# An S5 state-space mixer gated by an MLP: time steps on partitions replaced by states on partitions, a scan along time, and table GELU

## The chip, the cores and the metric

The kernel runs on one core of one Trainium2 chip. The metric is the device time of one execution in microseconds (us). The span of a profile is a little shorter than the time of the same execution (206.1 against 207.9 us in the changed kernel). TensorE does the matmuls (816 in the changed kernel's trace), VectorE, ScalarE and GpSimd the elementwise work (306, 163 and 142 instructions), SyncE issues most transfers (67 of the 77 listed there). In profile lines they are PE (with PEld for weight loads), DVE, ACT, POOL and SP. The program gives each engine its own queue of instructions in a fixed order, and an instruction that waits there holds up what stands behind it: in run 1 VectorE waited 8.2 us for a transpose that stood behind waiting matmuls in TensorE's queue. Every run is marked fast or slow. The slow ones are kept out of all ratios: one execution of run 5 (granted clock 0.73 instead of about 0.91), one of run 8 (210.74 us), and two of the kernel before (253.97 and 255.09 us). They are left out of the times quoted here, too.

## The reference

The input is 2048 tokens of 448 features. Both branches read the normalized token; the result is `x + s * silu(MLP)`.

```python
xn = layernorm(x)
# A: a diagonal complex recurrence over time, 448 states
Lam_bar = exp(dt * Lam)
Bu = xn @ (((Lam_bar - 1) / Lam)[:, None] * Bmat).T   # per token
h[t] = Lam_bar * h[t-1] + Bu[t]                     # 2048 steps
s = 2 * real(h @ Cmat.T) + xn * Dskip
# B: LayerNorm again, then 448 -> 1792 -> 448
m = gelu_tanh(layernorm(xn) @ w1 + b1) @ w2 + b2
out = x + s * silu(m)
```

## The kernel before

Both kernels work through groups of 512 tokens (four tiles of 128), and both fix the order of every engine's queue when they are built, from a list schedule with estimated durations. These parts matter.

```python
# recurrence inside 128 tokens: decay by tables, then a triangular matmul as prefix sum
def CS(t, ri):                       # x32 (16 tiles, real and imaginary)
    for pti in range(4):
        matmul(bk[:, pti*128:(pti+1)*128], Bs_sb[:, bb, ri, pti*128:...], Ub)   # 128x128
def CHAIN(t):                        # carry from tile to tile: four small GpSimd operations
    ...
def SE(t, ri):                       # eviction of each state block, carry added: 128 ScalarE operations
    for pt in range(4):
        act(S_sb[..., pt, ...], bk[:, pt*128:...], Identity, bias=vst[:, t, ri, pt:pt+1])

# GELU of each 128x512 block: ScalarE, then VectorE x3, ScalarE, VectorE
a  = act(bank, Identity, bias=b1)            # GA
u  = dve(a * a); q = dve(u * K + 1); w = dve(q * a)      # GU, GQ, GW
sg = act(w, Sigmoid, scale=2C)               # GS
gT = dve(sg * a)                             # GG

# end of a 128-token tile
sg2 = act(bank_o, Sigmoid); o = act(bank_o, Copy)        # SG
g   = dve(sg2 * o); t3 = dve(bank_y * g); out = dve(t3 + x)
# (LayerNorm, setup of the tables and the schedule are cut)
```

In what follows MM1 is the product with w1, MM2 that with w2, "state input" the product with B, and "output matmul" the product of the states with C.

## Time and profile before

| | before |
|---|---|
| time, median (range) | 251.84 us (251.17 to 253.85) |
| TensorE, VectorE, ScalarE busy | 182.4, 185.7, 181.0 us |
| ScalarE instructions | 417 |

The page of the profile gives the busy time of each engine with its share of the span. Below that it cuts the span into 40 slices (6.3 us each here). Each digit is a slice's busy share in tenths; the clock row is the clock that TensorE was granted.

```profile
PE 182.4 (72%) x1014; PEld 91.2 (36%) x1014; DVE 185.7 (74%) x498; ACT 181.0 (72%) x417; POOL 72.5 (29%) x224
...
PE   1003306299748652969996996899999899998894
...
DVE  4551895078426682999971999958799999999853
ACT  2599946337499945999947998868867968845431
...
PEclk9999999999997996779999899599999999999999
```

No engine is full on average. TensorE's row shows why averages mislead: it is nearly idle for seven slices, half full for another nine, and nearly full after that. The windows view gives the same by stretch: busy us and instruction count of each engine.

```profile
core 0: us, PE busy (x) PEld busy (x) DVE busy (x) ACT busy (x) POOL busy (x), PEclk, DMA share, GB/s
0.00:47.00 47.00, 11.11 (x102) 7.26 (x102) 25.50 (x70) 33.09 (x56) 14.93 (x66) 1.00 0.59 162
47.00:100.00 53.00, 33.52 (x153) 14.54 (x154) 30.00 (x81) 34.58 (x81) 24.63 (x75) 0.94 0.13 26
100.00:137.00 37.00, 32.11 (x173) 15.78 (x171) 30.40 (x75) 31.76 (x83) 19.13 (x47) 0.91 0.17 35
137.00:252.00 115.00, 105.63 (x591) 53.63 (x588) 99.78 (x273) 81.58 (x200) 13.84 (x36) 0.96 0.09 23
```

The groups of the page name a source line, the engine, output and inputs, then "busy us, mean ns", and last the idle time just before, with its releaser. These are the groups that the change removes or shrinks.

```profile
L777 ACT ACTIVATE sg_sb<-w_sb 128x512 bf16<-128x512 bf16 x56 | 33.5, 681 | 10.9 <-DVE w_sb L770 10.9
L746 ACT ACTIVATE a_sb<-bank,b1col 128x512 bf16<-128x512 f32 x56 | 37.8, 736 | 4.0 <-PE bank L737 4.0
...
L705 ACT ACTIVATE S_sb<-bank,vst 128x128 bf16<-128x128 f32 x128 | 37.6, 415 | 0.6 <-POOL vst L696 0.6
...
L754 DVE TENSOR_TENSOR u_sb<-a_sb 128x512 bf16<-128x512 bf16 x56 | 22.0, 421 | 13.6 <-ACT a_sb L746 13.5
...
L785 DVE TENSOR_TENSOR gT<-sg_sb,a_sb 128x512 bf16<-128x512 bf16 x56 | 21.6, 418 | 5.2 <-ACT sg_sb L777 5.1
L674 PE MATMUL bank<-Ub,Bs_sb 128*128 128x128 bf16 x128 | 12.6, 221 | 17.3 <-ACT S_sb L705 12.8
```

The two ScalarE steps of GELU and the state evictions are 109 us of ScalarE's 181.

### The profile page before, as it was taken

The page shows a single profiled execution, that of the slowest core. Times are in us where ns is not written, and L with a number is a line of the kernel's source. Part 1 is how long each engine was busy: PE and PEld are TensorE (multiplying, and loading weights), DVE is VectorE, ACT ScalarE, POOL GpSimd, SP SyncE. Part 2 cuts the span into 40 slices and gives each one's busy share as a digit, 9 for nine tenths or more (in the row PEclk, how much of TensorE's full clock was granted, in tenths as well). Part 3 has the DMA queues.
Part 4 walks back from the last instruction along what each step waited for, and adds up shares of the span by engine and source line. Part 5 has one row for each costly group of instructions (what it writes and reads, how often), then busy time and mean ns, then how long its engine had stood idle before and what let it go on. Part 6 is the DMA issues. An engine that isn't in the chain of part 4 may idle for free.

```text
span 251.9 us, 3616 instructions
## 1 busy us (share of the span) xinstructions
PE 182.4 (72%) x1014; PEld 91.2 (36%) x1014; DVE 185.7 (74%) x498; ACT 181.0 (72%) x417; POOL 72.5 (29%) x224
## 2 busy tenths in 40 slices
PE   1003306299748652969996996899999899998894
PEld 1002203134313321325553453345555455454452
DVE  4551895078426682999971999958799999999853
ACT  2599946337499945999947998868867968845431
POOL 7237000058312574134883331010011031010100
PEclk9999999999997996779999899599999999999999
DMA  6999123200123201112211122101000000000011
GB/s 194 284 328 252 23 43 62 46 0 0 21 42 65 42 0 23 21 21 44 62 39 21 42 42 43 39 3 39 18 21 0 18 1 22 0 18 21 18 36 36
DMA packets 24703, 12.92 MB, mean 51 GB/s; under 512 B 17958, under 2 KB 23883, under 8 KB 24684
## 3 DMA queue, kind: packets, MB, share of 16 engines
q1 hardware_dynamic: 24268, 11.09, 17.9%
q0 software_dynamic: 416, 1.61, 2.0%
q8 instruction: 8, 0.13, 0.2%
q14 instruction: 11, 0.09, 0.1%
HBM read 6.66 MB, written 1.84 MB: 34 GB/s over the span
## 4 chain that ended last, share of the span: by engine, by line
PE 34%; DVE 27%; POOL 14%; ACT 9%; issue 5%; DMA 5%; SPq 5%; ACTq 0%; DVEq 0%; POOLq 0%
PE bank L806 10%; PE bank L737 9%; PE bank L823 6%; SPq L178 5%; DMA Craw<-in_A_C_im_dram 4%; DVE w_sb L770 3%; PE bank L648 3%; DVE gT L785 3%; DVE h_sb L729 2%; POOL lnw L454 2%; ACT S_sb L705 2%; DVE u_sb L754 2%; DVE h_sb L725 2%; DVE m1s L721 2%; ACT xn_sb L487 2%
## 5 line engine op out<-in xcount | busy, mean ns | idle before, releaser
L737 PE MATMUL bank<-xn2T,w_sb 128*128 128x512 bf16 x224 | 57.9, 408 | 0.3 <-ACT a_sb L746 0.2
L806 PE MATMUL bank<-w_sb,gT 128*128 128x448 bf16 x224 | 46.3, 360 | 0.0
L777 ACT ACTIVATE sg_sb<-w_sb 128x512 bf16<-128x512 bf16 x56 | 33.5, 681 | 10.9 <-DVE w_sb L770 10.9
L746 ACT ACTIVATE a_sb<-bank,b1col 128x512 bf16<-128x512 f32 x56 | 37.8, 736 | 4.0 <-PE bank L737 4.0
L648 PE MATMUL bank<-BbT,xnT 128*128 128x512 bf16 x128 | 33.3, 408 | 10.0 <-DMA xn2T<-xn_sb 6.4
L688 POOL TENSOR_TENSOR chw<-Slast,vst 128x8 f32<-128x8 f32 x16 | 8.5, 532 | 109.2 <-ACT Slast L681 109.2
L705 ACT ACTIVATE S_sb<-bank,vst 128x128 bf16<-128x128 f32 x128 | 37.6, 415 | 0.6 <-POOL vst L696 0.6
L487 ACT ACTIVATE xn_sb<-x_all,lnw 128x448 bf16<-128x448 bf16 x32 | 23.6, 806 | 14.3 <-POOL lnw L475 14.3
L737 PEld LDWEIGHTS bank<-xn2T,w_sb 128*128 128x128 bf16 x224 | 22.5, 104 | 27.8 <-issue 6.0
L754 DVE TENSOR_TENSOR u_sb<-a_sb 128x512 bf16<-128x512 bf16 x56 | 22.0, 421 | 13.6 <-ACT a_sb L746 13.5
L823 PE MATMUL bank<-CT,h_sb 128*128 128x448 bf16 x128 | 29.0, 373 | 3.3 <-DVE t_sb L847 3.2
L806 PEld LDWEIGHTS bank<-w_sb,gT 128*128 128x128 bf16 x224 | 21.9, 100 | 20.4 <-issue 1.6
L785 DVE TENSOR_TENSOR gT<-sg_sb,a_sb 128x512 bf16<-128x512 bf16 x56 | 21.6, 418 | 5.2 <-ACT sg_sb L777 5.1
L674 PE MATMUL bank<-Ub,Bs_sb 128*128 128x128 bf16 x128 | 12.6, 221 | 17.3 <-ACT S_sb L705 12.8
L656 ACT ACTIVATE Bu_sb<-bank 128x512 bf16<-128x512 f32 x32 | 18.4, 645 | 7.1 <-PE bank L648 7.0
L648 PEld LDWEIGHTS bank<-BbT,xnT 128*128 128x128 bf16 x128 | 12.6, 103 | 25.3 <-issue 11.9
L770 DVE TENSOR_TENSOR w_sb<-q_sb,a_sb 128x512 bf16<-128x512 bf16 x56 | 21.3, 417 | 0.0
L837 ACT ACTIVATE sg<-bank 128x448 bf16<-128x448 f32 x16 | 8.9, 559 | 14.6 <-PE bank L809 14.4
L823 PEld LDWEIGHTS bank<-CT,h_sb 128*128 128x128 bf16 x128 | 12.5, 102 | 15.9 <-DVE t_sb L847 4.0
L674 PEld LDWEIGHTS bank<-Ub,Bs_sb 128*128 128x128 bf16 x128 | 9.2, 98 | 24.3 <-issue 10.6
L555 PE MATMUL bank<-identb,Craw 128*128 128x128 bf16 x32 | 4.3, 307 | 17.7 <-DMA Craw<-in_A_C_im_dram 17.7
L434 DVE BATCH_NORM_STATS2 lnst<-x_all 128x6 f32<-128x448 bf16 x16 | 8.8, 611 | 9.1 <-DMA xn2T<-xn_sb 9.1
(131 smaller groups left out, 275.9 us busy)
## 6 DMA issues: line engine op xcount, KB each, us to landing
x_all<-in_A_x_dram SPq DMA_DIRECT2D x4, 448.0 KB, 8.2
out_dram<-out_sb SPq DMA_DIRECT2D x16, 112.0 KB, 1.7
w_sb<-in_B_w_dram POOLq DMA_DIRECT2D x2, 784.0 KB, 11.1
w_sb<-in_B_w_dram SPq DMA_DIRECT2D x3, 448.0 KB, 4.0
Braw<-in_A_B_re_dram SPq DMA_DIRECT2D x1, 336.0 KB, 7.5
Braw<-in_A_B_im_dram SPq DMA_DIRECT2D x1, 336.0 KB, 11.7
Craw<-in_A_C_re_dram SPq DMA_DIRECT2D x1, 336.0 KB, 13.1
Craw<-in_A_C_im_dram SPq DMA_DIRECT2D x1, 336.0 KB, 11.0
```

The costliest lines, as they stand in the source:

```text
L487: kb.act(lambda e: e.activation(dst_ap, x_all[:, t, :], ACT.Identity, bias=nb, scale=rs), reads=[(KW, g), f"x_all{t}"], writes=[(dst_key, t)])
L648: kb.pe(lambda e: e.matmul(bk[:, 0:DP], xnT[:, gx, dti, tl * 128:(tl + 1) * 128], BbT[:, ri, dti, :], start=(dti == 0), stop=(dti == NDT - ...
L674: kb.pe(lambda e: e.matmul(bk[:, pti * 128:(pti + 1) * 128], Bs_sb[:, bb, ri, pti * 128:(pti + 1) * 128], Ub[:, :], start=True, stop=True) ...
L705: kb.act(lambda e: e.activation(S_sb[:, gbuf, pt, tl, ri, :], bk[:, pt * 128:(pt + 1) * 128], ACT.Identity, bias=vst[:, t, ri, pt:pt + 1], ...
L737: kb.pe(lambda e: e.matmul(bk[:, 0:512], w1_sb[:, dti, fi * 128:(fi + 1) * 128], xn2T[:, gbuf, dti, :], start=(dti == 0), stop=(dti == NDT ...
L746: kb.act(lambda e: e.activation(a_sb[:, ab, :], bk[:, 0:512], ACT.Identity, bias=b1col[:, 0, fi:fi + 1], scale=1.0), reads=[bkey, "b1col"] ...
L754: kb.dve(lambda e: e.tensor_tensor(u_sb[:, ub, :], a_sb[:, ab, :], a_sb[:, ab, :], ALU.mult), reads=[(f"a_sb{ab}", n)], writes=[(f"u_sb{ub ...
L770: kb.dve(lambda e: e.tensor_tensor(w_sb[:, wb, :], q_sb[:, qb, :], a_sb[:, ab, :], ALU.mult), reads=[(f"q_sb{qb}", n), (f"a_sb{ab}", n)], ...
L777: kb.act(lambda e: e.activation(sg_sb[:, sgb, :], w_sb[:, wb, :], ACT.Sigmoid, scale=GELU_2C), reads=[(f"w_sb{wb}", n)], writes=[(f"sg_sb{ ...
L785: kb.dve(lambda e: e.tensor_tensor(gT[:, gbuf, fi, :], sg_sb[:, sgb, :], a_sb[:, ab, :], ALU.mult), reads=[(f"sg_sb{sgb}", n), (f"a_sb{ab} ...
L806: kb.pe(lambda e: e.matmul(bk[:, 0:D], gT[:, gbuf, fi, tl * 128:(tl + 1) * 128], w2_sb[:, fi, :], start=(fi == 0), stop=False), reads=[(f" ...
L823: kb.pe(lambda e: e.matmul(bk[:, 0:D], h_sb[:, gbuf, pti, tl, ri, :], CT[:, ri, pti, :], start=first, stop=False), reads=[(hkey, g), "CT"] ...
```

## The change

The kernel is rewritten. States lie on partitions (448 states as three full tiles, real and imaginary, and one tile that holds the last 64 of both). The state is rotated by its own phase, so that the recurrence has a real factor and runs as one scan instruction along 512 time steps. GELU becomes one table instruction on two PSUM banks. SiLU is `0.5 m (1 + tanh(m/2))`; the 0.5 is folded into C and the skip term.

```diff
-matmul(bk[:, pti*128:...], Bs_sb[...], Ub)                        # 128 triangular matmuls
-act(S_sb[...], bk[:, pt*128:...], Identity, bias=vst[...])        # 128 evictions
+dve(tensor_tensor_scan(s_f[:, ub, ri, :], r.to_broadcast([128, 512]), v_sb[:, ub, ri, :],
+                       init, mult, add))                          # 28 scans
+act(s_b[:, ub, :, :], s_f[:, ub, :, :], Copy)                     # 1024 columns each
+dve: v = u*W before the scan, h = s*V after it (rotation in and out), six 1024-wide operations
-a = act(bank, Identity, b1); u, q, w = dve(...) x3; sg = act(w, Sigmoid); gT = dve(sg*a)
+act(gT[:, gb, 2*j:2*j+2, :], psum[:, b0:b0+2, :], Gelu_apprx_tanh)  # b1 is a row of w1
-sg2 = act(bank_o, Sigmoid); o = act(bank_o, Copy); g = dve(sg2 * o)
+th = act(psum[:, 6, :], Tanh, scale=0.5); g = dve((th + 1) * psum[:, 6, :])
+for i in range(4): sin and cos of 513 phases by ScalarE             # rotation tables, at the start
# ... the schedule, the loads and the LayerNorm are rewritten too (cut)
```

## The prediction

> **What bounds it now.** No engine is full over the 251.9 us span (page: TensorE 72%, VectorE 74%, ScalarE 72%). By the windows view: setup to 47 us (chain of waits: C load to 23 us, VectorE table doubling, TensorE transposes, a transposing DMA); 47-100 us TensorE busy 33.5 of 53 us (chain: LayerNorm scalars on GpSimd, then ScalarE); from 137 us a nearly full TensorE (105.6 of 115 us).
>
> **Removed** (grouped view): GELU's ScalarE copy, 4 VectorE operations and sigmoid (37.8 + 22.0 + 14.8 + 21.3 + 21.6 + 33.5 us) become 28 ScalarE GELUs of 1024 columns, estimated at 1.05 us: 29 us. The 128 triangular matmuls (about 7 us of pitch), 128 ScalarE state evictions (37.6 us), 16 of 128 B and 16 of 128 C matmuls go. Output sigmoid plus copy (17.9 us) becomes one tanh (9 us).
>
> **Added:** 28 scans of 512. [...] Six 1024-wide products per state-tile pair cost 0.685 us each (trace). A group's state work is about 22 us of VectorE, 10 us of ScalarE.
>
> **Per 512-token group afterwards**, at the pitch of before's chain (8 matmuls of 512 columns in 1.73 us, 14 of 448 in 2.65 us): TensorE 36 us, VectorE 29, ScalarE 26. TensorE, 143 us in all, limits the steady state.
>
> **Start.** TensorE begins real matmuls at 15-17 us instead of 47. But the static order alternates GELU and sine on ScalarE: 12 table loads instead of 5, 1.283 us each in the trace. ([...] before's timeline shows the activation 0.02 us after the load[...].) ScalarE's queue from the first GELU to group 0's last: 11 loads 14 us, GELUs 7, sines 5, rotation copies 6, B-product copies 3; so the first MM2 starts at about 53 us. In the static order the first scan's eviction stands behind the tanh of that MM2, so group 0's states then run through VectorE in sequence (28 us), and the first output matmul starts near 88 us. TensorE has gaps until then. It has about 112 us left there, 118 at the average granted clock of 0.95, plus a tail of 3 us.
>
> **Time:** 88 + 118 + 3 = about **209 us**, 8 in 10 within **195 to 224**. Chances: faster by over 2% 0.96, within 2% 0.03, slower 0.01.
>
> **Signs that it is right:** [...] a GELU pair at 1.05 us; 12 table loads, all before 55 us; first MM2 near 53 us; the first state eviction waiting for TensorE's MM2 by way of tanh; first output matmul near 88 us; TensorE over 90% busy from there, the chain mostly TensorE lines; VectorE 155-165 us busy in all, ScalarE about 120.
>
> **What would make it wrong.** (1) If loads or VectorE's tables let ScalarE run ahead or hold it up, the first output moves by 10 us. [...] (3) The order was planned without table loads; engines in a fixed order may stall on each other after the late start: 5 to 12 us more. (4) MM2 and the output matmul each have one PSUM bank, released by a VectorE operation behind scans: gaps on TensorE. [...]

What no trace had shown is cut: the time of one scan with its total, the sign and the risk that rested on it, a remark on table loads that was not counted, and a risk about the clock. The sums still hold the scans. VectorE's 22 us of state work per group are the products (about 14 us: six of 0.685 us for each of three tile pairs, somewhat fewer for the last) and seven scans as estimated. These are also in VectorE's 29 us per group, in its 155 to 165 us in all, and in the 28 us of group 0's states that lead to 88 us. The 1.05 us of a GELU pair is the author's estimate as well; the trace of before has a figure near it, 1.06 us for two 512-column evictions on ScalarE (L656, at 66.81 us).

## The result, and the profile after

| | before | after |
|---|---|---|
| time, median (range) | 251.55 us (251.17 to 253.85) | 207.76 us (207.45 to 207.90) |
| TensorE, VectorE, ScalarE busy | 182.4, 185.7, 181.0 us | 159.0, 154.5, 122.5 us |
| ratio | | 0.8248, 95% interval 0.8209 to 0.8286 |

A ratio is the mean time of one kernel's fast runs over that of the other's in the same rounds, so it is not quite the ratio of the medians. Before's median here is over four executions; the first table had three of them.

The page after, the same lines (slices of 5.15 us):

```profile
PE 159.0 (77%) x816; PEld 77.7 (38%) x816; DVE 154.5 (75%) x306; ACT 122.5 (59%) x163; POOL 44.1 (21%) x142
...
PE   0399339932900086999999999999999999979992
...
DVE  6877995756699986839695857999967999935333
ACT  2366999999223089859978666543677361681110
...
PEclk9999967996795558799999999999999999999998
```

TensorE starts its real work early, falls idle around 55 to 72 us, and is full from slice 17 on. The windows view has the same columns as before:

```profile
17.00:53.00 36.00, 21.22 (x86) 8.48 (x85) 26.42 (x75) 32.40 (x38) 5.21 (x18) 0.83 0.44 94
53.00:88.00 35.00, 16.22 (x57) 6.53 (x56) 29.42 (x56) 18.09 (x28) 22.30 (x63) 0.69 0.15 31
88.00:140.00 52.00, 52.00 (x276) 25.66 (x275) 39.72 (x60) 35.87 (x49) 9.07 (x37) 1.00 0.22 49
140.00:180.00 40.00, 40.00 (x218) 20.02 (x217) 35.49 (x54) 20.81 (x27) 2.67 (x9) 1.00 0.09 25
```

From 88 us TensorE has no gap and a granted clock of 1.00. VectorE is at 35.49 of 40 us in the last of these stretches, which becomes important below. The groups that answer to those of before, and the scan, with (x21) and without (x7) a start value that is carried from the group before:

```profile
L581 ACT ACTIVATE gT<-psum 128x1024 bf16<-128x1024 f32 x28 | 28.6, 1024 | 16.2 <-PE psum L574 16.0
...
L530 DVE TENSOR_TENSOR_SCAN s_f<-cw,cur,v_sb 128x512 f32<-128x512 f32 x21 | 25.9, 1270 | 0.6
...
L530 DVE TENSOR_TENSOR_SCAN s_f<-cw,v_sb 128x512 f32<-128x512 f32 x7 | 8.3, 1215 | 0.0
...
L593 ACT ACTIVATE th<-psum 128x448 f32<-128x448 f32 x16 | 8.6, 540 | 22.3 <-PE psum L591 22.3
...
L535 ACT ACTIVATE s_b<-s_f 128x1024 bf16<-128x1024 f32 x12 | 12.6, 1051 | 6.0 <-DVE s_f L530 6.0
```

A view of the instruction groups gives the activation table loads (count, busy us, mean ns). There are 12, as predicted, all before 49.3 us. None stands between GELU and tanh later. That no source line of tanh (L593) appears among them shows it.

```profile
L581 ACT ACT_TABLE_LOAD x6 | 7.7, 1283 | 0.1
L438 ACT ACT_TABLE_LOAD x3 | 3.8, 1283 | 1.6 <-DVE tb L436 1.5
L440 ACT ACT_TABLE_LOAD x2 | 2.6, 1283 | 0.0
L261 ACT ACT_TABLE_LOAD x1 | 1.3, 1283 | 1.6 <-PEq L675 1.6
```

The chain of waits, followed back from the last instruction and printed in order of time, tells which work the next one waited for. Each line is start us, length us, engine and line.

```profile
47.99 1.28 ACT L581
49.28 1.03 ACT gT L581
50.36 4.83 PE psum L589 x14
...
55.42 0.54 ACT th L593
55.96 0.95 ACT s_b L535
56.94 0.69 DVE pa L564
...
61.50 2.28 DVE s_f L530 x2
...
69.93 1.20 POOL lnw L354
71.20 1.04 POOL lnw L355
...
73.12 0.76 ACT xn_sb L369
...
78.04 2.48 DMA xnT<-xn_sb
...
80.66 2.52 PE psum L500 x8
83.18 3.70 PE psum L589 x14
...
90.52 1.32 PE psum L601 x7
```

Read from the top: a table load, the last GELU of group 0, the first MM2 at 50.36 us, its tanh, and directly behind it the first state's eviction. That is the sequence which the prediction had drawn. Then the chain leaves it. From 63.9 to 73.1 us it runs through GpSimd, which computes the LayerNorm scalars of group 1 in small steps, then through ScalarE's normalized tokens and a transposing DMA to the state input of group 1 at 80.66 us. From there every later piece down to the last matmul is TensorE, but for one GELU of 1.03 us at 183.56 us. The first output matmul (L601) starts at 90.5 us in this chain (90.4 us in the timeline, which is used below).

TensorE's own waits name another releaser for the largest gap, the gating of the first MM2, which frees the one PSUM bank of MM2:

```profile
PE psum L589 <- DVE g_sb L594: 16.7, 1, 16.7
PE psum L589 <- ACT gT L581: 8.4, 2, 7.3
```

So the trace offers several causes for the late start: table loads, one bank, the LayerNorm chain, VectorE's states. The experiments take them one by one.

### The profile page after: what moved, and what is told of

Read it like the earlier page. It is cut to its first block, busy times and chain, and to the rows that moved or that the text cites. A ratio compares the mean times of both kernels' runs of the same rounds, so it can differ in the third digit from the quotient of the medians.

```text
span 206.1 us, 2551 instructions
## 1 busy us (share of the span) xinstructions
PE 159.0 (77%) x816; PEld 77.7 (38%) x816; DVE 154.5 (75%) x306; ACT 122.5 (59%) x163; POOL 44.1 (21%) x142
## 4 chain that ended last, share of the span: by engine, by line
PE 61%; ACT 18%; POOL 6%; DMA 5%; DVE 4%; issue 2%; SPq 2%; DVEq 0%; ACTq 0%
PE psum L589 21%; PE psum L574 18%; PE psum L601 10%; PE psum L500 8%; DMA w_sb<-in_B_w_dram 4%; ACT L581 3%; ACT gT L581 2%; SPq L74 2%; ACT xn_sb L369 2%; ACT L438 2%; PE psum L603 2%; PE psum L591 1%; ACT tb L440 1%; PE psum L506 1%; ACT L440 1%
## 5 line engine op out<-in xcount | busy, mean ns | idle before, releaser
L589 PE MATMUL psum<-w_sb,gT 128*128 128x448 bf16 x224 | 50.7, 383 | 25.1 <-DVE g_sb L594 16.7
L574 PE MATMUL psum<-xn2T,w_sb 128*128 128x512 bf16 x224 | 53.9, 392 | 7.5 <-ACT gT L581 7.2
L589 PEld LDWEIGHTS psum<-w_sb,gT 128*128 128x128 bf16 x224 | 22.9, 105 | 50.4 <-issue 24.2
L581 ACT ACTIVATE gT<-psum 128x1024 bf16<-128x1024 f32 x28 | 28.6, 1024 | 16.2 <-PE psum L574 16.0
L574 PEld LDWEIGHTS psum<-xn2T,w_sb 128*128 128x128 bf16 x224 | 21.6, 101 | 33.7 <-ACT gT L581 8.2
L530 DVE TENSOR_TENSOR_SCAN s_f<-cw,cur,v_sb 128x512 f32<-128x512 f32 x21 | 25.9, 1270 | 0.6
L500 PE MATMUL psum<-xnT,BT 128*128 128x512 bf16 x96 | 23.3, 387 | 2.1 <-DMA xnT<-xn_sb 2.1
L601 PE MATMUL psum<-CT,h_sb 128*128 128x448 bf16 x112 | 23.8, 352 | 0.0
L593 ACT ACTIVATE th<-psum 128x448 f32<-128x448 f32 x16 | 8.6, 540 | 22.3 <-PE psum L591 22.3
L369 ACT ACTIVATE xn_sb<-x_all,lnw 128x448 bf16<-128x448 bf16 x24 | 16.7, 751 | 8.2 <-POOL lnw L358 8.2
L504 ACT ACTIVATE u_sb<-psum 128x1024 bf16<-128x1024 f32 x12 | 12.2, 1021 | 8.5 <-PE psum L500 6.6
L535 ACT ACTIVATE s_b<-s_f 128x1024 bf16<-128x1024 f32 x12 | 12.6, 1051 | 6.0 <-DVE s_f L530 6.0
L601 PEld LDWEIGHTS psum<-CT,h_sb 128*128 128x128 bf16 x112 | 11.0, 98 | 10.6
## 6 DMA issues: line engine op xcount, KB each, us to landing
out_dram<-o_sb SPq DMA_DIRECT2D x16, 112.0 KB, 1.7
```

What stands on the lines that cost most here:

```text
L369: act(lambda e: e.activation(dst, x_all[:, t, :], ACT.Identity, bias=nb, scale=rs), rd, [key], 0.66, prio)
L500: fns = [lambda e, ri=ri, d=d: e.matmul(psum[:, 4 + ri, :], BT[:, d, (ri * 3 + i) * 128:(ri * 3 + i + 1) * 128], xnT[:, gx, d, :], start=( ...
L504: act(lambda e: e.activation(u_sb[:, ub, :, :], psum[:, 4:6, :], ACT.Copy), ["ps4", "ps5"], [f"u{ub}"], 1.04, prio)
L530: dve(lambda e, ri=ri, init=init: e.tensor_tensor_scan(s_f[:, ub, ri, :], col(C_R, i).to_broadcast([128, 512]), v_sb[:, ub, ri, :], init, ...
L535: act(lambda e: e.activation(s_b[:, ub, :, :], s_f[:, ub, :, :], ACT.Copy), kS, [f"sb{ub}"], 1.04, prio)
L574: fns = [lambda e, k=k, d=d: e.matmul(psum[:, b0 + k, :], w1_sb[:, d, (2 * j + k) * 128:(2 * j + k + 1) * 128], xn2T[:, gx, d, :], start=( ...
```

## The experiments

All but the seventh are made from the changed kernel. For those whose edit is "order", the planned order of the changed kernel is kept for every engine and only the named operations, with what they depend on, are moved forward. Each ratio is to the kernel before in the same job. The changed kernel has 207.76 us and 0.8248.

### 1. All sines first

```diff
-tb = SB("tb", [128, 2, 3, TW]); g_sb = SB("g_sb", [128, 8, D])
+tb = SB("tb", [128, 4, 3, TW]); g_sb = SB("g_sb", [128, 5, D])   # room for four tables
+order: the 8 sines before the first GELU (3 table loads instead of 12)
```

> All eight sines stand before the first GELU on ScalarE (four table buffers instead of two, the order of everything else as in the changed kernel); correct output. Theory T (the table loads on ScalarE set the first MM2, and TensorE sets the rest): 3 table loads instead of 12, so 9 x 1.283 = 11.5 us less on ScalarE; the last GELU of group 0 ends near 41 us instead of 50.3, the first MM2 starts near 41-42 us, and the time falls by 7 to 10 us to 198-201 us. Rival R1 (VectorE's table building and state work set the start; ScalarE's loads hide behind it): first MM2 earlier, but the time falls by 3 us at most.

Measured: 208.53 us (207.35 to 208.62), ratio 0.8261. Nothing was gained, though ScalarE lost 9 loads (11.5 us). The first MM2 was at 51.0 us, not earlier. The waits of VectorE and of TensorE in this run show where the time went:

```profile
DVE BT L439 <- PE psum L431: 8.2, 1, 8.2
```
```profile
PE psum L614 <- ACT gT L621: 13.8, 2, 11.7
```

With the sines first, GELU came later, so TensorE's MM1 blocks waited for their banks. A transpose of B stood behind those blocks in TensorE's queue, and VectorE waited 8.2 us for it. The first scan started at 52.5 us; in the changed kernel it started at 50.5 us. The MM1 blocks themselves held the first MM2: one waited 11.7 us for the first GELU, which now stood behind the sines. Table loads alone are not the cause of the late start, and my expectation for this run was wrong.

### 2. The next group's LayerNorm early

```diff
+order: LayerNorm of group 1 forward; its first state input and four MM1 blocks before the second MM2
```

> The LayerNorm of group 1 and five blocks of TensorE work of group 1 (one input product, four first-MLP blocks, 8.6 us at full pitch) stand before the second MM2, which waited 16.7 us for VectorE; correct output. Theory T (TensorE is full from 81 us on; time falls by the work that moves into its gaps): 7 to 11 us less, 197-201 us, with the gap before the second MM2 mostly filled. Rival R2 (VectorE, 75% busy, sets the time): same time within 2 us, as VectorE has the same work.

Measured: 205.86 us (205.64 to 206.61), ratio 0.8172 (0.8131 to 0.8213): 2 us gained, at the edge of what the intervals tell apart. TensorE was busy 20.4 us between 50 and 81 us, against 11.9 in the changed kernel. It had gaps of 0.3 to 1.4 us between 81 and 120 us instead (34.3 of 39 us), on VectorE and ScalarE. Work moved forward, and most of it was paid back. The gain is what rival R2 (VectorE sets the time) had foretold, not theory T; run 4 tests R2 itself.

### 3. A second bank for MM2

```diff
-matmul(psum[:, 6, 0:D], gT[...], w2_sb[...])
+matmul(psum[:, 7 if t == 1 else 6, 0:D], gT[...], w2_sb[...])     # second MM2 alone
```

> The second MM2 writes another PSUM bank, so it need not wait for VectorE to release the first one; order unchanged, correct output. In the changed kernel that wait was TensorE's longest, 16.7 us. Theory T: what counts is the work that moves into the gap, one MM2 (2.84 us at full pitch, 3.9 us at the pitch of the one that then drops out before 87 us): 3 to 4.5 us less, 203.5-205 us. Rival R3 (a wait costs what it is long): 10 us less or more.

Measured: 207.63 us (206.78 to 208.64), ratio 0.8235: nothing, less than either expectation. The timeline of TensorE (start us, length us, then idle before in brackets) shows it at once:

```profile
55.51 2.81 PE L624 MATMUL psum<-w_sb,gT 128*128 128x448 bf16 x14
...
80.16 3.57 PE L534 MATMUL psum<-xnT,BT 128*128 128x512 bf16 x8 [21.65 <-DMA xnT<-xn_sb]
```

The second MM2 ran 17 us earlier and the wait of 16.7 us was gone. TensorE then waited 21.65 us for the same transposing DMA, to 80.16 us. The largest wait of the view was not a cost: taking it away only joined it to the next one.

### 4. A copy instead of the scan (wrong result)

```diff
-tensor_tensor_scan(s_f[...], r.to_broadcast(...), v_sb[...], init, mult, add)
+tensor_copy(s_f[...], v_sb[...])
```

> Wrong output on purpose: each of the 28 scans is replaced by a copy of the same shape [...], order unchanged: VectorE loses about 25 us of work. Theory T: after 81 us TensorE is the limit, so only the part of group 0's chain that is VectorE's counts (the two scans of the second state tile, and what follows from them): 2 to 5 us less, 203-206 us. Rival R2 (VectorE sets the time): 15 to 25 us less.

Measured: 204.04 us (203.65 to 204.58), ratio 0.8096. A copy took 0.422 us where the scan had taken 1.215 to 1.270. VectorE's busy time fell from 154.5 to 131.8 us, the time by 3.7 us, and the state input of group 1 started at 77.41 us instead of 80.66. So nearly all of the gain lies in the start (3.3 us), and the other 20 us or so of VectorE work had been covered by TensorE. R2, which asked for 15 to 25 us, is ruled out for the kernel as a whole. The check of the output passed this run too, though its result is wrong. The check does not notice a missing scan, and "correct" in this document means no more than that a run passed it.

The trace also tells beside what LayerNorm's scalars on GpSimd take so long. In the chain of the changed kernel, two small operations of 128x8 took 1.20 and 1.04 us from 69.93 us on, while the two scans ran on VectorE (69.90 to 72.2 us). The same two lines of source in this run, where the scan is a copy, in the timeline of GpSimd:

```profile
68.13 0.45 POOL L383 TENSOR_TENSOR lnw<-lnw 128x8 f32<-128x8 f32 x1
68.67 0.25 POOL L384 TENSOR_SCALAR lnw<-lnw 128x8 f32<-128x8 f32 x1
```

In both timelines such operations took 0.20 us beside VectorE's LayerNorm statistics, and 0.5 to 0.7 us beside its products of two tensors, ending about when these ended. What makes them longer is not seen in a trace. GpSimd's group of LayerNorm scalars, with the carry work between, took 8.9 us in the changed kernel (64.14 to 73.08) and 7.4 us here (62.33 to 69.77). The difference of 1.5 us is that of the two lines (2.24 against 0.70 us). So the scans delayed this chain twice: by their own time on VectorE, and by the longer GpSimd operations beside them. My prediction had not counted the second.

### 5. Every scan twice

```diff
+tensor_tensor_scan(dump[:, ri, :], ...same operands...)
 tensor_tensor_scan(s_f[:, ub, ri, :], ...)
```

> Each of the 28 scans is preceded by one more of the same size into a buffer that nobody reads: about 35 us more on VectorE (154.5 to about 189 us busy), order unchanged, correct output. Theory T: group 0's chain before 81 us grows by the two to four extra scans that lie on it (2.5 to 5 us), and VectorE's work per group rises from about 29 to 38 us against TensorE's 36, so it begins to limit: 6 to 16 us more, 213-223 us. Rival R2 (VectorE already sets the time): 30 us more or beyond.

Measured: fast runs of 230.77, 233.10 and 233.93 us, ratio 0.9223 (0.9151 to 0.9295): 25 us more than the changed kernel, between the two expectations. The work added is about 35 us, worked out from 28 scans of 1.215 to 1.270 us. The slack is thus small: most of what is added to VectorE is paid. This agrees with the window of the changed kernel in which VectorE was busy 35.49 of 40 us. The added scans may also have made GpSimd's operations longer: two of them took 2.24 us beside two scans in the changed kernel, and 0.70 us beside the copies of run 4; without a fast trace of this run, the 25 us cannot be divided.

### 6. Sigmoid instead of tanh

```diff
-act(th, psum[:, 6, :], Tanh, scale=0.5); g = (th + 1) * psum
+act(th, psum[:, 6, :], Sigmoid);         g = (th * 2) * psum
```

> Only the SiLU goes back to a sigmoid (scaled so that the output stays correct), everything else and the order as in the changed kernel. The built program then has 31 table loads instead of 12, 19 more x 1.283 = 24 us on ScalarE, which has room (122.5 of 206 us busy). Theory T: ScalarE's added time is mostly hidden, but each load delays a tanh-like step or a GELU that releases a PSUM bank for TensorE: 4 to 14 us more, 211-221 us. Rival R4 (the loads are free because ScalarE has slack): within 2 us. Rival R5 (ScalarE sets the time): 24 us more.

Measured: 212.07 us (211.61 to 212.79), ratio 0.8411: 4.3 us more. There were 31 loads instead of 12 (19 x 1.283 = 24.4 us of ScalarE). Most is hidden, since ScalarE has room (122.5 of 206.1 us busy in the changed kernel). Tanh rather than sigmoid is worth about 4 us here because it needed no load beside GELU (none after 49.3 us in the changed kernel).

### 7. The kernel before, with table GELU and tanh alone

```diff
 # in the kernel before
-GA (Identity), GU, GQ, GW, GS (Sigmoid), GG
+act(gT[:, gbuf, fi, :], bank, Gelu_apprx_tanh, bias=b1)
-act(sg2, bank_o, Sigmoid); g = sg2 * o
+act(sg2, bank_o, Tanh, scale=0.5); g = (sg2 + 1) * o      # 0.5 in C and the skip term
```

> The kernel before with two parts of the change alone: GELU as one table instruction (bias inside it) and SiLU by tanh; its start, its chunked recurrence with triangular matmuls and its scheduler stay; correct output. VectorE loses 80 us, ScalarE about 38 us. Theory T (the start at 47 us stays, then TensorE is the limit with about 157 us of full-pitch work, and the recurrence's chain leaves some gaps): 212-225 us, so that this part gives most of the gain and the scan with the shorter start the rest. Rival R6 (the gain is the recurrence's new layout): above 235 us.

Measured: 226.79 us (226.34 to 228.25), ratio 0.9008. That is 1.8 us above the expected range. So this part alone gives 25 of the 44 us, and the new layout of the states with its other start and order the remaining 19. The windows show TensorE at 121.0 of 125 us from 100 us on; the nearly full stretch had begun at 137 us in the kernel before. The setup to 47 us was untouched by it.

### 8. TensorE kept busy in its gaps

```diff
+18 idle 128x512 matmuls before the first MM2, 60 before the second
```

> The changed kernel with 18 idle matmuls of 512 columns (results unused) on TensorE before the first MM2 and 60 before the second, to keep it busy in its gaps; order of the rest unchanged, correct output. If the low granted clock after a gap (0.5 at 50-53 and 73-78 us) comes from the gap, the two MM2s take 2.8 us each instead of 5.0 and 5.6 us, and the granted clock there is near 1. Theory T: 2 us from the first MM2 and 1 to 2 us from the slow matmuls at 80.7-87 us lie on the chain: 2.5 to 4.5 us less, 203-205 us. Rival R7 (the clock is not a matter of the gaps): same matmul times, and 0 to 1 us more.

Measured: fast runs of 205.37, 205.55 and 207.35 us, ratio 0.8171 (0.8117 to 0.8226), whose interval still overlaps that of the changed kernel. The profiled span was 2.3 us shorter at a mean clock of 0.967 against 0.914. The state input at 79.57 us took 1.89 us instead of 2.52, and the MM2 after it 2.81 instead of 3.91. Both MM2s that still had 3.4 to 3.7 us of idle time just before them took 4.2 to 4.3 us. The state input came after 3.52 us of idle time and yet ran at full pace, so the length of the gap just before does not settle the clock:

```profile
79.57 1.89 PE L539 MATMUL psum<-xnT,BT 128*128 128x512 bf16 x8 [3.52 <-ACT s_b L576]
```

So part of the start, about 2 us of the span, is TensorE at a lower clock after gaps. In the changed kernel the first MM2, after 7.27 us of idle time, was granted 0.50 from 50.36 to 53.77 us and 0.77 from there to 55.30 us. The second, after 16.72 us of idle time, was granted 0.50 from 72.96 to 78.3 us. They took 4.83 and 5.38 us, against 2.81 us for the MM2 of run 8 at 81.29 us, at a granted clock of 1.00 (79 to 88 us). What sets the moment at which the clock comes back was not shown.

### 9. Sines first, and the transposes of B first

```diff
 # as run 1
+order: all transposes of B, and the first state input, before the first MM1 in TensorE's queue
```

> The eight sines before the first GELU (3 table loads instead of 12), as in the run that had that alone, and in addition all seven transposes of B with their copies, and the first state-input product, moved in TensorE's order ahead of the first MLP product. So the scan no longer waits behind MLP products in TensorE's queue. The theory that was formed after that run failed (the start is a braid of in-order queues; loads and queue order must be mended together): first MM2 at 43 to 47 us, first scan at 46 to 49 us instead of 52.5, full TensorE stretch from about 72 to 76 us, total 199 to 204 us. Rival (the start is set by VectorE's own work, the tables and the first group's state products, whatever the queues do): the first scan stays near 52 us and the total stays within 3 us of the changed kernel, 205 to 209 us.

Measured: 206.36 us (204.39 to 207.24), ratio 0.818. One half of the expectation held: the first scan moved to 47.6 us, because VectorE no longer waited behind MM1. The other half did not. MM2 started at 51.6 us, and the first state's eviction, which still stood behind the tanh of that MM2 in ScalarE's queue, came at 55.05 us. VectorE waited 4.25 us for it. The 5 us won against run 1 were lost at the next place in a queue.

### 10. All reorderings of the start together

```diff
 # as run 9, with the second bank of run 3
+order: LayerNorm of group 1 as in run 2; second MM2, first state input and four MM1 blocks of
+       group 1 before the third MM2; their GELUs before the eviction of the third state
```

> All reorderings of the start at once: the eight sines first, the transposes of B first, the LayerNorm of group 1 and its first MLP blocks before the second MM2, the second MM2 in another PSUM bank. The order of the rest, its arithmetic and its instruction counts are as in the changed kernel. If the start is a braid whose strands must be loosened together, this gains more than the sum of the single ones (about 0, 2 and 0 us): 188 to 198 us, with TensorE above 75% busy already between 55 and 80 us; VectorE's about 155 us of work plus its waits then becomes the next limit. If VectorE's work sets the start, 203 to 207 us, and VectorE is above 85% busy between 30 and 85 us.

Measured: 205.03 us (203.81 to 205.39), ratio 0.8129 (0.8086 to 0.8172). It beats both kernels: 1.4% below the changed kernel by the ratios, whose intervals do not overlap. Its strands alone had gained 1.4 us (run 9), 1.9 us (run 2) and 0.1 us (run 3), 3.4 us in all. Together they gained 2.7 us: not more than their sum, against my expectation. The time lies in the range of the rival, that VectorE's work sets the start, but its sign did not hold either: VectorE was busy 43.5 of 55 us (79%, not over 85%) between 30 and 85 us. TensorE was busy 16.7 of 25 us between 55 and 80 us (6.9 in the changed kernel), and then only 31.5 of 40 us between 80 and 120 us (39.3 in the changed kernel). VectorE had a single wait of 7.0 us (total, times, longest):

```profile
DVE pa L617 <- ACT s_b L588: 12.9, 5, 7.0
```

The LayerNorm that I had moved forward now stood, with the tanh, ahead of the first state's eviction in ScalarE's queue.

### 11. States sooner

```diff
 # as run 10, and order:
+tables of state tiles 2 and 3 behind the states of tiles 0 and 1; evictions ahead of LayerNorm and tanh
+LayerNorm of group 2 behind all states of group 0
```

> The combined reordering, with what its trace showed still to wait undone too, by order alone: the rotation tables of state tiles 2 and 3 are built after the states of tiles 0 and 1 instead of before them; the eviction of each state stands in ScalarE's queue ahead of the next group's LayerNorm and of the tanh (in the combined run VectorE stood 7.0 us for it at 51 to 58 us); the LayerNorm statistics of group 2 stand behind all states of group 0; the first four MLP blocks of group 1 stand ahead of the state input that they had waited behind; 5 table loads instead of 12. If these places in the queues are what holds the start: first scan at about 36 to 40 us, the last state of group 0 ready at 68 to 73 us instead of 84, full TensorE stretch from about 66 to 72 us, total 190 to 199 us. If the start is held by something that order does not touch, such as VectorE's total work in it: 202 to 206 us.

Measured: 228.72 us (227.85 to 229.00), ratio 0.9058. This is a fault of my reordering: GpSimd, which issues the load of w2, had been given LayerNorm work ahead of it that waited for VectorE (GpSimd was busy 0.57 us from 20 to 40 us and not at all from 40 to 55 us). TensorE stood 18.7 us for w2 and the first MM2 ran at 76.8 us. The run says nothing about the theory. It says how much one place in a queue can hold up.

### 12. The first eviction ahead

```diff
 # as run 10, and order:
+eviction of the first state before LayerNorm and tanh in ScalarE's queue
+LayerNorm of group 2 behind all states of group 0; four MM1 blocks of group 1 before its state input,
+their GELUs in pairs before the evictions of the third and the fourth state
```

> The run before this one failed (228.7 us), and its trace says why: by the reordering GpSimd issued the load of w2 only after LayerNorm work that waits for VectorE, so the first MM2 waited 18.7 us for w2 and ran at 76.8 us. So it says nothing of the theory. This run keeps the combined reordering of the 205.0 us run, with w2 loaded as before, and changes only what that run's trace showed waiting: the first state's eviction stands ahead of the next LayerNorm and the tanh in ScalarE's queue (VectorE had stood 7.0 us for it); group 2's LayerNorm statistics stand behind all states of group 0; the first four MLP blocks of group 1 stand ahead of the state input that they had waited behind. If the places in the queues hold the start: VectorE's wait of 7.0 us at 51 to 58 us is gone, the last state of group 0 is ready at 72 to 77 us instead of 84 to 85, total 196 to 202 us. If order does not hold it: 203 to 207 us.

Measured: 210.18 us (209.62 to 210.97), ratio 0.8338. The wait that was aimed at was gone, from 7.0 to 0.9 us. The last state of group 0 was ready at 79.8 us; in the changed kernel it was at 83.8. Yet the time was 5 us longer than in run 10, beyond both expectations. The longest wait of the same pair of lines was now 5.1 us, for the third state's eviction, which stood behind two GELUs that I had placed there and that waited for TensorE:

```profile
DVE pa L629 <- ACT s_b L600: 16.5, 7, 5.1
```

The third MM2 waited 7.5 us for the gating of the first, which I had left behind group 2's statistics in VectorE's queue. So order does hold part of the start, and each change of order had a price elsewhere. What the shortest start would be was not found; twelve runs leave that open.

## Why the prediction was right, point by point

The time was 207.8 us where 209 had been predicted. It is right as a sum, and only partly by its mechanism.

| term | predicted | measured |
|---|---|---|
| first output matmul | 88 us | 90.4 us |
| TensorE's work from there | 118 us | 112.0 us (90.4 to 202.4) |
| tail | 3 us | 3.7 us |
| sum | 209 us | 206.1 us span, 207.8 us time |

- **Steady state: right.** TensorE limits it, at the pitch read from before's trace (8 matmuls of 512 columns in 1.73 us, 14 of 448 in 2.65 us), and is 100% busy from 88 to 180 us. The average granted clock of before, 0.95, should not have been charged on it: the clock was 1.00 there, and the lower values lie in the start. That was 6 us too much.
- **Unit costs: right within about 3% where they stand.** A GELU pair took 1.024 us (1.05 predicted); 12 loads, each of 1.283 us, and the GELU behind the last of them started 0.01 us after it; VectorE 154.5 us (155 to 165), ScalarE 122.5 us (120). A scan took 1.215 us without and 1.270 us with a carried start value, against 0.69 us for a product of two fp32 tensors of that size in the kernel before; the estimate for it had been shown by no trace.
- **VectorE's slack: wrong in size.** I gave VectorE 29 us of work in 36 us of TensorE per group, so a slack of 7 us. Run 5 added about 35 us and cost 25: about 233 us, where theory T of that run had 213 to 223. The sum of the work was right (75.2 of 92 us between 88 and 180 us, which is 29.4 per 36), but it is uneven: 89% busy between 140 and 180 us. So VectorE's waits leave less room than the sum says. It did not spoil the result because VectorE's work came to no more than was predicted (154.5 us, for 155 to 165).
- **The start: right in its length, in part by luck, and wrong in part of its cause.** The first MM2 was at 50.4 us for 53, and the first eviction did stand behind its tanh, as predicted. It cost 2.2 us. "ScalarE's queue from the first GELU" was predicted to set the first MM2; run 1 took 11.5 us of loads out of that queue and the first MM2 stayed at 51.0 us, because MM1 blocks now waited for GELUs behind the sines. (The transposes of B behind MM1 held the first scan, as run 9 showed: without them it came 5 us earlier, and the first MM2 still at 51.6 us.) That group 0's states "then run through VectorE in sequence (28 us)" held (56.9 to 83.8 us). But the states did not set the first output matmul: they were ready at 83.8 us, and it came at 90.4 us because TensorE, full since 80.66 us, had other work before it in its queue. That this falls near the predicted 88 us is luck. TensorE's full stretch was opened at 80.66 us by the next group's LayerNorm, by GpSimd, ScalarE and a DMA. Run 3 showed that the wait on the PSUM bank, which the list of risks had named, costs nothing while that chain is later. Run 4 showed that a shorter scan moves the chain by 3.3 us and the whole kernel by 3.7, since LayerNorm's statistics share VectorE with the states, and its scalars on GpSimd took longer beside VectorE's scans (2.24 us for two operations, against 0.70 us beside the copies).
- **The static order: the risk that was named was real.** "Engines in a fixed order may stall on each other after the late start" was guessed at 5 to 12 us more. Of the eight changes to the start (runs 1 to 3 and 8 to 12), none gained more than 2.7 us. So none of the places that were tried holds the start alone. That places in the queues hold other engines up is what runs 1, 9, 10 and 12 show; how much a good order could gain is open. The rival, that VectorE's own work sets most of the start, is not ruled out: VectorE was busy 27.65 of 31 us (89%) between 50 and 81 us in the changed kernel, and run 4, which took scans out of it, moved the state input 3.3 us forward.

The gain itself is divided by run 7: 25 us for the two activations, 19 us for the rest. The two parts were only run in this one division.

## What to carry to other kernels

When each engine's queue has a fixed order, the longest wait in a profile need not be a cost (here 16.7 us cost nothing): follow the chain past it, and test it by taking it away, before counting on it. Work that is removed from one engine during the start may only uncover the next wait, as in runs 1 and 9, so look for what stands behind the removed work in all of them. For a steady state with one full engine, sum that engine's work at its measured full-clock pitch, and test the slack of the second busiest engine, which here was much less than its busy time suggested.
